# Loading a tap filter and k's first chunk ahead of ssm_k, and running two tap products during that load

## Chip, cores, metric

One core of one Trainium2 chip. Times are device microseconds of one execution (lower is better); a trace's own clock starts a little later, so the profiled spans are some 1.8 us shorter than the times. All ratios below compare runs on the same chip in the same rounds, and use only the runs whose state is fast (a run more than 1.5% above the fastest of its kernel counts as slow). Start times are read from one profiled execution of each kernel, some of them on different chips. The verdict "same" means within 2%.

## The reference, cut to what matters

```python
# S = 2048 tokens, D = 512 channels, 4 taps
k_shift[t] = sum over j of k[t - j] * shift_k[:, j]      # the tap filter
kv  = k_shift * v
y   = irfft( rfft(kv, 2S) * rfft(ssm_k, 2S) )[:S] + kv * ssm_D
h   = x + layernorm(x) * y                               # then an MLP with 512 -> 1376 -> 512
```

The kernel does the Fourier transforms as matmuls. `ssm_k` has to be transposed into rows (`kfl`) and put through a first DFT stage (into `a1k`); the tap filter is a product with diagonal matrices (`wdiag`) accumulated in PSUM, then multiplied by v in place (`vT`). Only when all of k·v is there can its own transposes begin. From there on this change touches nothing.

## The kernel before

```python
sk = ...;   nc.sync.dma_start(out=sk, in_=A_ssm_k)          # 2 MB, first on SP's ring
wsh = ...;  nc.scalar.dma_start(out=wsh, in_=A_shift_k)     # 4 KB, ACT's ring
for c in range(4):                                          # k and v, transposed by the DMA, behind ssm_k
    nc.sync.dma_start_transpose(out=kT[c], in_=k_d[...])
    nc.sync.dma_start_transpose(out=vT[:, :, ...], in_=v_d[...])
# ... cut: VectorE computes the angles of the sine tables (add, wrap), ScalarE the sines
for rg in range(4):                                         # GpSimd, when the filter is there
    nc.gpsimd.tensor_tensor(out=wdiag[:, rg], in0=ident, in1=wsh[:, rg], op=mult)

def to_rows(src, q, fl, eng):                # one group of 8 transposes, and its copy out of PSUM
    pst = psum.tile(...)                     # pool of four buffers, shared by all of the below
    for i in range(8):
        nc.tensor.transpose(out=pst[:, 0, i, :], in_=src[:, :, :, 8 * q + i], identity=ident)
    copy(eng, fl[:, :, :, 8 * q:8 * q + 8], pst[:, 0])

def taps(c, h):                              # one tap product: 8 matmuls of 512 columns, then times v
    ps = bank2("pkv")
    for i in range(2):
        for j in range(4):
            nc.tensor.matmul(out=ps[:, i, :], lhsT=wdiag[:, 2 * h + i, j, :], rhs=kT[c][...])
    nc.vector.tensor_tensor(out=vv, in0=ps, in1=vv, op=mult)

for q in range(8):
    to_rows(ssm_k, q, kfl, "DADADADA"[q])    # D: VectorE copies, A: ScalarE copies
for gb in range(8):                          # eight rounds
    taps(gb // 2, gb % 2)
    stage1(kfl, a1k, gb, ("AA", "AD")[gb % 2])   # 64 small matmuls, two evictions
    if gb in (0, 2, 4): cc_part()                # a sine table on ScalarE
# ... cut: the transposes of k·v and everything after
```

## Time and profile before

| | before |
|---|---|
| time, median of 3 runs | 221.04 us (220.21 to 221.72) |
| span of the profiled execution, mean granted TensorE clock | 218.5 us, 0.997 |
| first transpose of ssm_k / stage 1 / first transpose of k·v | 9.23 / 18.01 / 38.61 us |

The prediction shows the chain of waits and the loads. Three more views of this kernel are needed later: the page's shares of the chain that ended last, its row of the granted TensorE clock (one digit for a fortieth of the span, 9 is 90% or more), and, in the timeline, VectorE's work on the tables (start, duration, engine, line, operation).

```profile
PE 77%; DVE 11%; DMA 5%; ACT 2%; issue 2%; SPq 0%; DVEq 0%; ACTq 0%
```

```profile
PEclk9999999999999999999999999999999999999998
```

```profile
4.52 0.90 DVE L180 TENSOR_SCALAR w_ts<-w_ts 128x1408 int32<-128x1408 int32 x1
5.33 0.82 DVE L189 TENSOR_TENSOR w_ts<-w_ta 128x640 int32<-128x640 f32 x1
...
6.18 0.49 DVE L180 TENSOR_SCALAR w_ts<-w_ts 128x640 int32<-128x640 int32 x1
```

Of the 5% of DMA, 4% is the load of ssm_k (8.46 us). VectorE's tables run beside that load; they end at 9.35 + 1.23 = 10.58, and VectorE's first copy of kfl follows at 10.50 (neighbours overlap by a little). So VectorE is only just ready when the first eight transposes are.

### The profile page before, as it was taken

Reading aid. Unit: us, or ns where it says so; the run is one execution under the profiler, and the core shown is the slowest. Engines: PE = TensorE matmul, PEld = TensorE weight load, DVE = VectorE, ACT = ScalarE, POOL = GpSimd, SP = SyncE. Lnnn points to the kernel's source line nnn. Section 1 sums busy time; section 2 is a strip of 40 time slices with the busy share of each in tenths; the row PEclk is TensorE's granted clock in tenths of the full one; section 3 lists DMA queues with packets and bytes.
Section 4 is the critical chain, followed back from the end, with each engine's and each line's share of the span. In section 5 each row is a group of like instructions: output and inputs, shape, how many; then the busy total and the mean of one; then the engine's idle time right before and its main releaser. Section 6 shows DMA issues by size and latency. Waiting matters only on the chain.

```text
span 218.5 us, 5526 instructions
## 1 busy us (share of the span) xinstructions
PE 197.3 (90%) x2299; PEld 139.4 (64%) x2299; DVE 144.6 (66%) x226; ACT 116.6 (53%) x175; POOL 79.1 (36%) x120
## 2 busy tenths in 40 slices
PE   0389789999997999998999889999999999999992
PEld 0385444999986899995998844645646644444451
DVE  7975657886688899998495992976395480243031
ACT  2977847745598688884897128401550046106400
POOL 4299982000001899997648702100202001002000
PEclk9999999999999999999999999999999999999998
DMA  6999950000000004827941898594344430020012
GB/s 187 315 210 197 158 115 3 3 6 0 0 3 3 4 0 130 226 98 188 196 63 36 252 134 168 94 166 98 81 84 82 96 80 1 18 54 24 3 48 48
DMA packets 49512, 20.07 MB, mean 92 GB/s; under 512 B 44400, under 2 KB 47952, under 8 KB 49488
## 3 DMA queue, kind: packets, MB, share of 16 engines
q1 hardware_dynamic: 46816, 18.18, 40.7%
q10 hardware_dynamic: 2672, 1.54, 2.6%
q8 instruction: 18, 0.29, 0.5%
q14 instruction: 6, 0.05, 0.1%
HBM read 7.08 MB, written 2.10 MB: 42 GB/s over the span
## 4 chain that ended last, share of the span: by engine, by line
PE 77%; DVE 11%; DMA 5%; ACT 2%; issue 2%; SPq 0%; DVEq 0%; ACTq 0%
PE ps2m L603 18%; PE ps1m L586 18%; PE pkv L304 7%; PE psy L390 6%; PE pst L250 5%; PE pz L574 5%; DVE a1x L242 4%; DMA sk<-in_A_ssm_k_dram 4%; PE ps2k L282 3%; PE ps2k L284 3%; PE u L282 3%; PE u L284 3%; PE psi L510 3%; PE ps L266 3%; ACT ax L240 2%
## 5 line engine op out<-in xcount | busy, mean ns | idle before, releaser
L588 ACT ACTIVATE h1T<-ps1m 128x512 bf16<-128x512 f32 (+1 forms) x44 | 26.0, 596 | 56.2 <-PE ps1m L586 56.2
L586 PE MATMUL ps1m<-xT,w 128*128 128x512 bf16 (+1 forms) x176 | 39.0, 379 | 0.9 <-issue 0.6
L603 PE MATMUL ps2m<-w,h1T 128*128 128x512 bf16 (+3 forms) x187 | 39.4, 367 | 0.0
L606 DVE SCALAR_TENSOR_TENSOR o<-ps2m,rstd,xh 128x512 bf16<-128x512 f32 (+1 forms) x17 | 12.2, 719 | 32.3 <-PE ps2m L603 30.1
L586 PEld LDWEIGHTS <-w 128*128 128x128 bf16 (+1 forms) x176 | 17.4, 100 | 21.4 <-issue 1.1
L603 PEld LDWEIGHTS <-h1T 128*128 128x128 bf16 (+1 forms) x187 | 17.9, 98 | 19.2
L380 POOL TENSOR_TENSOR t<-usb,kf 128x320 fp32r<-128x320 f32 x32 | 28.3, 925 | 2.0 <-ACT usb L376 1.7
L380 DVE TENSOR_TENSOR t<-u,kf 128x704 fp32r<-128x704 f32 x32 | 26.7, 885 | 3.1 <-ACT usb L376 3.0
L460 POOL TENSOR_SCALAR rstd<-mv 128x4 f32<-128x4 f32 x8 | 2.3, 284 | 68.2 <-DVE mv L458 68.2
L456 DVE BATCH_NORM_STATS2 st<-xh 128x6 f32<-128x512 bf16 x32 | 19.7, 679 | 0.0
L240 ACT CAST kf<-psy 128x512 fp32r<-128x512 f32 x30 | 17.6, 645 | 2.0 <-PE psy L390 0.3
L574 PEld LDWEIGHTS pz<-ecore,ax 32*128 32x128 f32 x512 | 15.0, 186 | 3.4 <-issue 2.1
L574 PE MATMUL pz<-ecore,ax 32*128 32x128 f32 (+7 forms) x512 | 15.8, 273 | 1.1 <-ACT ax L240 1.1
L556 DVE TENSOR_TENSOR qT<-pz,qT 128x1024 bf16<-128x1024 f32 x8 | 9.8, 1223 | 10.5 <-PE pz L574 6.6
L390 PE MATMUL psy<-t,ipos 128*128 128x512 f32 x48 | 16.0, 393 | 0.0
L240 ACT CAST a1k<-ps 128x1024 fp32r<-128x1024 f32 x12 | 12.4, 1071 | 6.3 <-PE ps L266 6.3
L510 PE MATMUL psi<-dre,kf 128*128 128x256 f32 x64 | 15.5, 286 | 0.0
L250 PE MATMUL pst<-ident,sk 128*128 128x128 bf16 x64 | 6.5, 276 | 9.8 <-DMA sk<-in_A_ssm_k_dram 9.2
L304 PE MATMUL pkv<-kT,wdiag 128*128 128x512 bf16 x64 | 15.2, 381 | 0.0
L510 PE MATMUL psi<-dim,kf 128*128 128x256 f32 x64 | 15.2, 280 | 0.0
L240 ACT CAST ax<-psi 128x1024 fp32r<-128x1024 f32 x13 | 12.4, 1019 | 4.6 <-DVE st L456 3.0
L307 DVE TENSOR_TENSOR vT<-pkv,vT 128x1024 bf16<-128x1024 f32 x8 | 9.8, 1224 | 7.0 <-PE pkv L304 6.8
(115 smaller groups left out, 396.8 us busy)
## 6 DMA issues: line engine op xcount, KB each, us to landing
sk<-in_A_ssm_k_dram SPq DMA_DIRECT2D x1, 2048.0 KB, 8.5
xh<-in_A_q_dram SPq DMA_DIRECT2D x16, 128.0 KB, 3.0
out_dram<-o SPq DMA_DIRECT2D x60, 32.0 KB, 1.6
w<-in_B_w_dram SPq DMA_DIRECT2D x1, 1376.0 KB, 6.4
w<-in_B_w_dram ACTq DMA_DIRECT2D x1, 1280.0 KB, 6.3
xh<-xT SPq DMA_TRANSPOSE x8, 3.2
w<-in_B_w_dram ACTq DMA_DIRECT2D x1, 96.0 KB, 6.2
kT<-in_A_k_dram SPq DMA_TRANSPOSE x4, 6.1
```

The source lines that it names most:

```text
L240: nc.scalar.copy(out=o, in_=i)
L250: nc.tensor.transpose(out=pst[:, 0, i, :], in_=src[:, :, :, 8 * q + i], identity=ident[:])
L282: nc.tensor.matmul(out=ps[:, kk, :], lhsT=at_k1(w_re, k1), rhs=a_in[:, k1, :], start=True, stop=False, skip_group_check=True)
L304: nc.tensor.matmul(out=ps[:, i, :], lhsT=wdiag[:, 2 * h + i, j, :], rhs=kT[c][:, 2 * h + i, 16 - j:CH + 16 - j], start=(j == 0), stop=(j = ...
L380: eng.tensor_tensor(out=t[:, :, j, :], in0=in0.unsqueeze(1).to_broadcast([P, 2, n, 2]), in1=kfr[:, :, j, ks], op=ALU.mult)
L390: nc.tensor.matmul(out=psy[:], lhsT=m_[:], rhs=t_.rearrange("p j k -> p (j k)"), start=first, stop=not first)
L456: nc.vector.bn_stats(out=st[:, i, :], in_=src[:, i, :])
L510: nc.tensor.matmul(out=ps[:, i // 2, i % 2, :], lhsT=kf[:, c, 4 * m:4 * m + 4, :].rearrange("p r k -> p (r k)"), rhs=d[:].rearrange("p d a ...
L574: nc.tensor.matmul(out=pz[:, rg, 32 * jl:32 * (jl + w)], lhsT=ax[rows, 64 * rho + n2, :, :].rearrange("p d g -> p (d g)"), rhs=ecore[q][ro ...
L586: nc.tensor.matmul(out=ps1[:fsz, :].rearrange("p (i t) -> p i t", i=4), lhsT=w1[:, c, fc * P:fc * P + fsz], rhs=hT[sc][:, :, c, :], start= ...
L588: nc.scalar.activation(out=h1T[:fsz, fc, :], in_=ps1[:fsz, :], func=ACT.Relu)
L603: nc.tensor.matmul(out=ps2[:, 0:w], lhsT=h1T[:ksz, fc, i * P:(i + 1) * P], rhs=w2[:ksz, fc, ds], start=(fc == 0), stop=(fc == NFC - 1))
```

## The change

TensorE is idle until ssm_k has landed. The intent is to use that time: bring the filter (4 KB) and k's first chunk (512 KB) in before ssm_k, run that chunk's two tap products while ssm_k loads, park them in SBUF (`ahead`), and multiply them with v later from there. Two of the eight tap products, 1.84 us each, should so leave the critical path.

```diff
-    nc.sync.dma_start(out=sk[:], in_=A_ssm_k...)
-    nc.scalar.dma_start(out=wsh[:], in_=A_shift_k...)
+    nc.sync.dma_start(out=wsh[:], in_=A_shift_k...)
         if c == 0:
             nc.sync.dma_start_transpose(out=kT[c][:, :, 16:CH + 16], in_=k_d[0:CH, :])
+            nc.sync.dma_start(out=sk[:], in_=A_ssm_k...)
# GpSimd: wdiag right after ident (before: after the two memsets f2hi, f2lo)
+    ahead = slotA.tile([P, DC, CH], F32, tag="A", name="ahead")
+    for h in range(2):
+        nc.scalar.copy(out=ahead[:, 2 * h:2 * h + 2, :], in_=taps_mm(0, h))
     for q in range(8):
         to_rows(skv, q, kfl, "DADADADA"[q])
+        if q in (4, 6):
+            taps_mul(ahead[:, q - 4:q - 2, :], 0, q // 2 - 2)
     for gb in range(8):
-        taps(gb // 2, gb % 2)
+        if gb >= 2:
+            taps_mul(taps_mm(gb // 2, gb % 2), gb // 2, gb % 2)
         stage1(kfl, a1k, gb, ("AA", "AD")[gb % 2])
```

(`taps_mm` and `taps_mul` are the two halves of `taps`. The cut says in words what moved on GpSimd.)

More of the change, by code (lines that the diff above doesn't have):

```diff
@@ L94 @@
     sk = early.tile([P, DC, S], BF16, name="sk")
-    nc.sync.dma_start(out=sk[:], in_=A_ssm_k.rearrange("(c p) t -> p c t", p=P))
     wsh = consts.tile([P, DC, KS], BF16, name="wsh")
-    nc.scalar.dma_start(out=wsh[:], in_=A_shift_k.rearrange("(r p) j -> p r j", p=P))
+    nc.sync.dma_start(out=wsh[:], in_=A_shift_k.rearrange("(r p) j -> p r j", p=P))
     dtab = consts.tile([P, 64, DC], BF16, name="dtab")
@@ L111 @@
             nc.sync.dma_start_transpose(out=kT[c][:, :, 16:CH + 16], in_=k_d[0:CH, :])
+            nc.sync.dma_start(out=sk[:], in_=A_ssm_k.rearrange("(c p) t -> p c t", p=P))
         else:
@@ L153 @@
                             base=0, pattern=[[-1, P]], channel_multiplier=1)
+    for rg in range(DC):
+        nc.gpsimd.tensor_tensor(out=wdiag[:, rg, :, :], in0=ident[:].unsqueeze(1).to_broadcast([P, KS, P]),
+                                in1=wsh[:, rg, :].unsqueeze(2).to_broadcast([P, KS, P]), op=ALU.mult)
     n1c = early.tile([P, 1], F32, name="n1c")
@@ L219 @@
         nc.gpsimd.memset(f[:], 0.0)
-    for rg in range(DC):
-        nc.gpsimd.tensor_tensor(out=wdiag[:, rg, :, :], in0=ident[:].unsqueeze(1).to_broadcast([P, KS, P]),
-                                in1=wsh[:, rg, :].unsqueeze(2).to_broadcast([P, KS, P]), op=ALU.mult)
     nc.gpsimd.tensor_copy(out=f1hi[:, 0:64], in_=f1f[:])
@@ L285, in stage2, with taps_mm, taps_mul @@
                              skip_group_check=True)
+    def taps_mm(c, h):
+        ps = bank2("pkv")
+        for i in range(2):
+            for j in range(KS):
+                nc.tensor.matmul(out=ps[:, i, :], lhsT=wdiag[:, 2 * h + i, j, :],
+                                 rhs=kT[c][:, 2 * h + i, 16 - j:CH + 16 - j], start=(j == 0), stop=(j == KS - 1))
+        return ps[:]
+    def taps_mul(src, c, h):
+        vv = vT[:, 2 * h:2 * h + 2, CH * c:CH * c + CH]
+        nc.vector.tensor_tensor(out=vv, in0=src, in1=vv, op=ALU.mult)
+    ahead = slotA.tile([P, DC, CH], F32, tag="A", name="ahead")
+    for h in range(2):
+        nc.scalar.copy(out=ahead[:, 2 * h:2 * h + 2, :], in_=taps_mm(0, h))
     kfl = early.tile([P, 64, 2, 64], BF16, name="kfl")
@@ L297 @@
     a1k = slotA.tile([P, 64, 256], F32R, tag="A", name="a1k")
-    def taps(c, h):
-        ps = bank2("pkv")
-        for i in range(2):
-            for j in range(KS):
-                nc.tensor.matmul(out=ps[:, i, :], lhsT=wdiag[:, 2 * h + i, j, :],
-                                 rhs=kT[c][:, 2 * h + i, 16 - j:CH + 16 - j], start=(j == 0), stop=(j == KS - 1))
-        vv = vT[:, 2 * h:2 * h + 2, CH * c:CH * c + CH]
-        nc.vector.tensor_tensor(out=vv, in0=ps[:], in1=vv, op=ALU.mult)
     for gb in range(8):
-        taps(gb // 2, gb % 2)
+        if gb >= 2:
+            taps_mul(taps_mm(gb // 2, gb % 2), gb // 2, gb % 2)
         stage1(kfl, a1k, gb, ("AA", "AD")[gb % 2])
```

## The prediction

> **What bounds the kernel now.** I read the chain of work that ended last first, in order of time, because it says which work of the start is on the path. Columns: start, duration (us), what.
>
> ```profile
> 0.72 8.46 DMA sk<-in_A_ssm_k_dram
> 9.23 4.25 PE pst L250 x40
> 13.51 1.24 DVE kfl L242
> 14.79 1.56 PE pst L250 x16
> 16.35 1.73 PE pkv L304 x8
> 18.08 0.61 PE ps L266 x64
> 18.70 1.84 PE pkv L304 x8
> ...
> 26.14 1.76 issue
> ...
> 37.33 1.24 DVE vT L307
> 38.61 6.01 PE pst L250 x64
> ```
>
> Everything waits for ssm_k until 9.2. Then come 64 transposes of it (L250), then eight rounds of tap products (pkv, L304) and the first DFT stage (ps, L266), then at 38.61 the transposes of k·v. From there on the program is unchanged and TensorE is its chain nearly throughout (PE 90% busy on the page; loads wait for PE, not PE for loads), so I count what the change does to the time 38.61 and carry that to the end one to one. One round takes 1.84 + 0.61 = 2.45 us with TensorE never idle, except once: 1.76 us of "issue" near 26.
>
> Next the list of DMA issues (last column: us from issue to landing) and the timeline of the start.
>
> ```profile
> sk<-in_A_ssm_k_dram SPq DMA_DIRECT2D x1, 2048.0 KB, 8.5
> kT<-in_A_k_dram SPq DMA_TRANSPOSE x4, 6.1
> wsh<-in_A_shift_k_dram ACTq DMA_DIRECT2D x1, 4.0 KB, 8.8
> ```
>
> ```profile
> 1.25 7.79 SPq L111 DMA_TRANSPOSE kT<-in_A_k_dram  x1
> 9.64 4.85 POOL L222 TENSOR_TENSOR wdiag<-ident,wsh 128x512 bf16<-128x512 bf16 x4 [6.34 <-DMA wsh<-in_A_shift_k_dram]
> 10.50 1.21 DVE L242 COPY kfl<-pst 128x1024 bf16<-128x1024 bf16 x1
> 13.51 1.22 DVE L242 COPY kfl<-pst 128x1024 bf16<-128x1024 bf16 x1 [0.20 <-PE pst L250]
> 16.39 1.01 ACT L240 COPY kfl<-pst 128x1024 bf16<-128x1024 bf16 x1 [1.13 <-PE pst L250]
> 18.76 1.99 ACT L240 CAST a1k<-ps 128x1024 fp32r<-128x1024 f32 x2 [1.36 <-PE ps L266]
> 20.62 1.25 ACT L184 ACTIVATE c2c<-w_tc,hbi,hsc 128x1024 fp32r<-128x1024 int32 x1
> ```
>
> The tap filter (4 KB) arrives only with ssm_k, and k's first chunk, stuck behind ssm_k, lands at 1.25 + 10.2 = 11.45 (the 10.2 is the largest landing time in the view of tile kT). So today no tap product can run early. But the first tap product (16.35) already covers a wait: the last copy of kfl ends only at 16.39 + 1.01 = 17.40, and stage 1 needs all of kfl. It costs about 18.08 - 17.5 = 0.5 us, not 1.73.
>
> **What the Trainium skill says.** (1) "DMA: Bandwidth & Descriptors", Queues, rings and completion order: each DMA engine serves one ring in order and takes turns between rings. The trace agrees: the 4 KB filter on ACT's ring landed 8.8 us after issue, beside ssm_k's 8.5. Put first on SP's ring the filter is early, and k's chunk really goes ahead of ssm_k. (2) "TensorE: Matmul & The Clock Gate", Part 1: an idle array starts at 1.2 GHz, 426.7 ns per 512-column matmul, for at least about 3.4 us. In this trace warm tap matmuls go at 1.84/8 = 230 ns; the first 40 transposes took 106 ns each, and the 64 later ones 6.01/64 = 94, which is compatible but no proof. (3) "Advanced Engine Details and Errata", ISA Cache: 256 instructions a line, two lines. The trace has an instruction queue with 18 packets of 16 KB, one of them in 25 to 26 us, just ahead of the 1.76 us "issue" gap; I read that gap as a late instruction block. (4) "GPSIMD Engine Reference", 1. Specifications: GpSimd shares SBUF access with VectorE. One wdiag product beside a VectorE operation took 1840 ns, the others 1035.
>
> **The change part by part.**
>
> *a. Loads.* Bytes ahead of ssm_k grow by k's chunk (512 KB). The same two transfers were both done at 11.45 before, so with the order turned round ssm_k lands at about 11.5: by rates, the DMA windows show 0.39 MB/us for ssm_k and at best 0.29 for transposes, so 0.52/0.29 = 1.8 us for the chunk and 0.5 to 0.7 us for the small filter and D packets, 9.2 + 2.4 = 11.6. Cost: +2.3 us. All later transposes stay where they are: the total of bytes ahead of them is the same (about 2.7 us each, the last landing at 24.5 + 5.4 = 30).
>
> *b. The early tap products.* The filter lands near 3, wdiag is four products of 1.03 to 1.84 us, so done at 7.5 to 9; k's chunk lands near 6. Sixteen matmuls warm are 3.7 us, cold 6.8. I take 10 to 12 cold ones: 12 x 0.427 + 4 x 0.23 = 6.0, ending near 12.0. So TensorE, not ssm_k, may be what starts the transposes, at about T = 12.0. That is +2.8 against 9.23. ScalarE's two copies (1.0 each) fall to 11 to 13, then the table (1.25); kfl copies wait little for that.
>
> *c. Transposes of ssm_k.* They went from 9.23 to stage 1 at 18.01, 8.8 us. After: the built program's waits show that groups 2, 4 and 6 each wait for VectorE's copy of the group two before (the early tap products hold two of the four PSUM buffers when these groups are assigned). One such step is copy 1.22 + transposes 0.8 + hand-overs 0.15 = 2.17 us (13.51 to 15.68 in the trace is one). So: first copy at T + 1.0, third group's copy at T + 5.4, ended T + 6.6; now the first multiplication with v (1.22 us, as for the PSUM form at L307) stands in VectorE's queue ahead of the copy of group 6, which runs T + 7.85 to T + 9.1. The last ScalarE copy ends about T + 9.45. Stage 1 starts at T + 9.5 = 21.5. Before it was 18.01: +3.5 in all.
>
> *d. The rounds of stage 1.* Two tap products are gone (each 1.84 us of TensorE), but ScalarE's and VectorE's evictions take over at the head. From stage 1's start t0, with copies of 1.0 (ACT), 1.22 (DVE), table 1.15: first two evictions end t0 + 2.75, table 3.9, third 4.9. Tap product of round 2 waits for the first (1.8, ends 3.7), stage 1 of round 2 follows (ends 4.35), tap product of round 3 waits for the eviction at 4.9. That is 0.6 + 0.6 us of new idle time on TensorE. From round 3 on it is again 2.45 to 2.55 a round: stage 1 of round 7 starts at t0 + 16.95, the last multiplication with v ends at t0 + 18.4. Before, without the issue gap: 38.61 - 18.01 - 1.76 = 18.85. So only 0.4 us of the 1.84 is gained here, since ScalarE (12 copies and 3 tables, 15.8 us) is nearly as long as TensorE (6 x 1.84 + 8 x 0.61 = 15.9).
>
> *e. The issue gap.* The instruction block is needed at the same place in the program, the end of round 3. From the start of round 2 to there it had 3.2 us before and took 5; now it has about 3.7, and fewer transposes are still in flight. I put the gap at 0.6 of 1.76 (0 to 1.8).
>
> Sum: transposes of k·v start at 12.0 + 9.5 + 18.4 + 0.6 = 40.5, against 38.61: +1.9 us. 221.04 + 1.9 = 222.9.
>
> **The rivals.** *R1, the intended one:* tap products are free under the load, ssm_k is delayed little, and 2 x 1.84 us or a bit more vanish. For it: TensorE, idle until 9.23, has the room. Against it: the 0.5 MB must go through the same 16 DMA engines, busy 90% in the second slice of the page. It would give 217.5 to 219. *R2: the load order decides* and costs more than is won, my view: +1.9. *R3: cold TensorE and crowded GpSimd.* wdiag comes only at 9 to 10 and all sixteen matmuls run cold; transposes start at 13.5 to 14 and the whole is 225 to 226. For it: the 1840 ns product and VectorE being busy 2 to 10.5 us. Against: GpSimd has nothing else to do from 3.3 to 9.6. *R4: the issue gap as it was, or gone:* +-1 us around any of these. *R5: the load is hidden anyway,* the multiplications from SBUF fall into VectorE's idle time and all is a draw: 221.
>
> **Range and chances.** Uncertain are T (+-0.9), the copies' order (+-0.5), the gap (+-0.8), and runs (220.2 to 221.7 before). Together about 1.6 us for 8 in 10, widened a little downward for R1: 220.5 to 225.0. Over 2% faster is below 216.6, which needs more than even R1 gives: 0.02. Over 2% slower is above 225.5, R3 with the gap: 0.07. Within: 0.91.
>
> **What would show it.** Right if ssm_k lands near 11.5 and its first transpose starts at 11.5 to 12.5; a tap matmul takes about 0.43 us at first; the multiplication stands ahead of group 6's copy; stage 1 starts near 21.5; TensorE has two gaps of about 0.6 us before rounds 2 and 3; the k·v transposes start near 40.5 and everything later is shifted by the same amount. Wrong if ssm_k lands before 10.5 (R1), if wdiag ends after 9.5 (R3), if the first two rounds of stage 1 don't wait for ScalarE, or if the shift at the k·v transposes is not the shift at the end, in which case a later stage has slack I did not see.

## The result, and the profile after

| | before | after | predicted |
|---|---|---|---|
| median (range), 4 runs each | 221.38 us (220.21 to 221.87) | 223.75 us (223.52 to 223.98) | 222.9 (220.5 to 225.0) |
| profiled span, mean granted clock | 218.5 us, 0.997 | 222.0 us, 0.992 | |
| ssm_k's first transpose | 9.23 | 12.30 | 12.0 |
| stage 1 starts | 18.01 | 21.91 | 21.5 |
| k·v's first transpose | 38.61 | 42.09 | 40.5 |

The ratio is 1.0115 (95% interval 1.0071 to 1.0159): slower by about 1%, verdict "same". Ratios here and below are the mean time of one kernel's fast runs over that of the other's of the same rounds, so not quite the ratio of the quoted medians. From k·v's first transpose to the end both traces take 179.9 us, so all of the 3.5 us between the two traces arises in the first 42 us.

First the page's shares of the chain that ended last and its clock row, of the kernel after.

```profile
PE 80%; DVE 15%; issue 2%; ACT 2%; POOL 0%; DVEq 0%; POOLq 0%; ACTq 0%
```

```profile
PEclk9999799999999999999999999999999999999999
```

The load has gone from the chain, and VectorE's share rose from 11 to 15%. The fifth slice (22.2 to 27.8 us) ran at a reduced TensorE clock. The chain in order of time (start, duration, what) shows where:

```profile
2.75 1.75 DVE w_ts L192
...
12.42 1.23 DVE w_tc L183
13.65 1.14 DVE kfl L242
...
14.84 0.87 PE pst L250 x8
...
21.91 1.10 PE ps L266 x51
...
24.13 2.44 PE pkv L292 x8
...
29.90 1.49 issue
```

Before, the chain began with "DMA sk". Now, after some small operations of GpSimd and VectorE, it runs along VectorE's tables until the first copy of kfl at 13.65. ssm_k came late too, but what started the copies last was VectorE. Then come steps of a VectorE copy and eight transposes (14.84, and again at 17.01), then stage 1 and a tap product that takes 2.44 us (1.84 before) in the slice of the low clock, and an issue gap of 1.49.

From the list of DMA issues (last column: us from issue to landing), and from the timeline, one line each:

```profile
sk<-in_A_ssm_k_dram SPq DMA_DIRECT2D x1, 2048.0 KB, 8.6
```

```profile
6.19 6.28 PE L292 MATMUL pkv<-kT,wdiag 128*128 128x512 bf16 x16 [6.19 <-DMA kT<-in_A_k_dram]
```

ssm_k was issued at 3.58 (the timeline has that line too) and landed at 3.58 + 8.6 = 12.2; the filter took 2.0 us, where it took 8.8 before. The sixteen early matmuls really ran under the load, from 6.19 to 12.47, but cold: their weight loads start every 0.43 us.

Last, the timeline of GpSimd and VectorE at the start, after (queried in narrow windows, so that the four products show one by one; here in order of start):

```profile
2.75 1.74 DVE L192 TENSOR_TENSOR w_ts<-w_ta 128x1408 int32<-128x1408 f32 x1
3.10 2.29 POOL L155 TENSOR_TENSOR wdiag<-ident,wsh 128x512 bf16<-128x512 bf16 x1
4.53 1.61 DVE L183 TENSOR_SCALAR w_ts<-w_ts 128x1408 int32<-128x1408 int32 x1
5.36 1.68 POOL L155 TENSOR_TENSOR wdiag<-ident,wsh 128x512 bf16<-128x512 bf16 x1
6.06 1.66 DVE L192 TENSOR_TENSOR w_ts<-w_ta 128x640 int32<-128x640 f32 x1
7.00 1.62 POOL L155 TENSOR_TENSOR wdiag<-ident,wsh 128x512 bf16<-128x512 bf16 x1
7.75 1.21 DVE L183 TENSOR_SCALAR w_ts<-w_ts 128x640 int32<-128x640 int32 x1
8.58 1.28 POOL L155 TENSOR_TENSOR wdiag<-ident,wsh 128x512 bf16<-128x512 bf16 x1
...
13.57 1.22 DVE L242 COPY kfl<-pst 128x1024 bf16<-128x1024 bf16 x1
```

Read the ends, start plus duration: VectorE 4.49, GpSimd 5.39, VectorE 6.14, GpSimd 7.04, VectorE 7.72, GpSimd 8.62, VectorE 8.96, GpSimd 9.86. They alternate strictly, and each GpSimd product ends 0.90 us after the VectorE operation ahead of it. I read this as the two engines taking turns, whole instruction by whole instruction, so that an operation's duration in the trace includes its wait for the other engine. This is how VectorE's wrap went from 0.90 to 1.61 us, the add from 0.82 to 1.66, the second wrap from 0.49 to 1.21, and a small one after them from 0.23 to 1.01: +3.05 us in all, and the first copy of kfl came at 13.57 instead of 10.50, +3.07. It fits the Trainium skill, "SBUF — State Buffer", Who interferes with whom: there a VectorE instruction in a 2-port mode, or one with two SBUF inputs beside a GpSimd one that reads SBUF, contends with GpSimd, and the one that issues second "fully blocks". Before, wdiag came after 9.64, when most of VectorE's table work was done: only its first product met a table operation (it took 1.84 us and ended at 11.48, again 0.90 after that operation's end at 10.58), the other three took 1.03 each, and VectorE's copies out of PSUM beside them kept their 1.21 to 1.23 us.

### The profile page after: what moved, and what is told of

The parts are those of the page before. It is cut to its first block, busy times and chain, and to the rows that moved or that the text cites. A ratio compares the mean times of both kernels' runs of the same rounds, so it can differ in the third digit from the quotient of the medians.

```text
span 222.0 us, 5528 instructions
## 1 busy us (share of the span) xinstructions
PE 201.2 (91%) x2299; PEld 141.1 (64%) x2299; DVE 147.5 (66%) x226; ACT 118.8 (54%) x177; POOL 83.8 (38%) x120
## 4 chain that ended last, share of the span: by engine, by line
PE 80%; DVE 15%; issue 2%; ACT 2%; POOL 0%; DVEq 0%; POOLq 0%; ACTq 0%
PE ps2m L612 17%; PE ps1m L595 17%; PE psi L519 7%; PE psy L399 7%; PE pz L583 5%; PE pkv L292 5%; DVE a1x L242 4%; PE pst L250 4%; PE ps2k L282 3%; PE ps2k L284 3%; PE u L282 3%; PE u L284 3%; PE ps L266 3%; DVE kfl L242 2%; DVE w_ts L192 2%
## 5 line engine op out<-in xcount | busy, mean ns | idle before, releaser
L615 DVE SCALAR_TENSOR_TENSOR o<-ps2m,rstd,xh 128x512 bf16<-128x512 f32 (+1 forms) x17 | 12.2, 719 | 32.0 <-PE ps2m L612 29.2
L292 PE MATMUL pkv<-kT,wdiag 128*128 128x512 bf16 x64 | 18.2, 439 | 6.5 <-DMA kT<-in_A_k_dram 6.2
L292 PEld LDWEIGHTS <-wdiag 128*128 128x128 bf16 x64 | 6.6, 109 | 15.1 <-POOL wdiag L155 5.4
L240 ACT CAST a1k<-ps 128x1024 fp32r<-128x1024 f32 x12 | 12.4, 1073 | 5.4 <-PE ps L266 5.4
```

Of the source, the lines that this page charges most:

```text
L240: nc.scalar.copy(out=o, in_=i)
```

## The experiments

Twelve runs were made, in three batches, each batch on one chip. "Stage 1" and "k·v" are start times in the profiled execution.

| run | base and edit | stage 1 | k·v | median us | ratio to before (95%) |
|---|---|---|---|---|---|
| a0_after_again | after, unaltered | 22.4 | 42.4 | 223.6 | 1.0136 (1.0089, 1.0182) |
| e1_order_only | before, load order alone | 21.7 | 43.9 | 223.49 | 1.0142 (1.0091, 1.0192) |
| e2_free_load | after, ssm_k not behind k | 22.2 | 41.8 | 222.95 | 1.0112 (1.0067, 1.0157) |
| e5_filter_early | before, filter early alone | 21.96 | 41.8 | 222.82 | 1.0062 (1.0031, 1.0093) |
| e3_buffers | after, PSUM buffers in turn | 20.38 | 40.2 | 221.94 | 1.0049 (1.0026, 1.0071) |
| e4_round0 | after, ScalarE relieved | 22.4 | 41.8 | 224.23 | 1.0178 (1.0129, 1.0227) |
| c1_no_waits | e3, multiplications last | 19.55 | 40.1 | 222.27 | 1.0067 (1.0040, 1.0094) |
| c2_keep_warm | c1, 12 idle matmuls | 20.2 | 40.9 | 223.5 | 1.0117 (1.0064, 1.0171) |
| p1_before_pad | before, 15 idle transposes | 17.8 | 36.89 | 219.47 | 0.9963 (0.9935, 0.9990) |
| a1_after_pad | after, 15 idle matmuls | 22.16 | 43.1 | 226.22 | 1.0261 (1.0201, 1.0320) |
| c3_no_waits_pad | c1, 28 idle matmuls | 20.27 | 38.17 | 221.8 | 1.0051 (1.0027, 1.0075) |
| p2_before_warm | before, 58 idle transposes | 17.8 | 37.67 | 223.12 | 1.0105 (1.0059, 1.0152) |

The theories: **(A)** the load order sets the start; **(B)** something else would hold the start even with a free load; **(C)** the assignment of PSUM buffers costs a wait in every second group; **(D)** ScalarE holds the first rounds; **(E)** the issue gap is a late block of instructions, tied to a place in the program.

### The change again, on another chip

> The changed kernel again, unaltered, so that the two padded runs have it beside them on the same chip: ratio to before 1.008 to 1.015, first transpose of k*v at 41.5 to 42.5, issue gap at the end of round 3 between 0.9 and 1.8 us.

1.0136, beside 1.0115 in the first measurement. The first one was no accident, and all six runs again had a mean clock below full (see below).

### A against B: the loads

**e1_order_only.** The kernel before, with the order of loads alone.

```diff
-    nc.sync.dma_start(out=sk[:], in_=A_ssm_k...)
-    nc.scalar.dma_start(out=wsh[:], in_=A_shift_k...)
+    nc.sync.dma_start(out=wsh[:], in_=A_shift_k...)
             nc.sync.dma_start_transpose(out=kT[c][:, :, 16:CH + 16], in_=k_d[0:CH, :])
+            nc.sync.dma_start(out=sk[:], in_=A_ssm_k...)
```

> The kernel before with the new load order alone (filter first, k's first chunk ahead of ssm_k); no early tap products, wdiag at its old place. If the load order is the cost: ssm_k's first transpose at about 12.2 us, 8.8 us to stage 1 as before, first transpose of k*v near 41.4 (before 38.61, after 42.09), time about 2.8 us above before (ratio 1.013), so at or above the changed kernel. If the load order is hidden by something else (rival): ratio 1.000 to 1.004. If the early tap products win much and only the load order loses (rival), this run is more than 2 us above the changed kernel.

Transposes of ssm_k start at 12.62, and the kernel is 1.4% slower than before, about 3.1 us: as slow as the whole change. So the new order of loads is enough for the whole cost, and the early tap products won back nothing that the times show. But this edit also brings the filter early, so it does not tell A from B: wdiag ran from 3.29, and VectorE's wrap took 1.61 us here too. (The profiled execution was the slowest of the six, 225.43 us, so its k·v start of 43.9, for 41.4 expected, overstates the delay.)

**e2_free_load.** The whole change, but with ssm_k right behind the filter. The early tap products then have no k to read, so they read a constant tile; they are the same matmuls with wrong values, on purpose (the output stayed within the tolerance, which says nothing here).

```diff
     nc.sync.dma_start(out=wsh[:], in_=A_shift_k...)
+    nc.sync.dma_start(out=sk[:], in_=A_ssm_k...)
+    kfake = kvp.tile([P, 256], BF16, name="kfake");  nc.vector.memset(kfake[:], 0.125)
...
-                                 rhs=kT[c][:, 2 * h + i, 16 - j:CH + 16 - j], ...)
+                                 rhs=kfake (broadcast to 512 columns) if c == 0 else kT[c][...], ...)
```

> Wrong result on purpose: the changed kernel with ssm_k issued ahead of k's first chunk again and the early tap products reading a constant tile, so they cost no load. The load order as the only cost would give a first transpose of ssm_k at 9.5 and a time near 221.0, some 2.7 us below the changed kernel. My theory is that TensorE, cold, is nearly as late as the load: early products from 5.5 (wdiag) for 16 x 0.43 us, end near 12, so ssm_k's transposes start at 11.7 to 12.3 and the time is only 0 to 0.7 us below the changed kernel.

Taking ssm_k's delay away gained nothing: ratio 1.0112 (all six runs at a mean clock of 0.985 or less), and stage 1 at 22.2. In its timeline the transposes wait for VectorE instead:

```profile
13.91 1.22 DVE L244 COPY kfl<-pst 128x1024 bf16<-128x1024 bf16 x1
...
15.18 1.60 PE L252 MATMUL pst<-ident,sk 128*128 128x128 bf16 x16 [1.78 <-DVE kfl L244]
```

They started at 11.83, when the cold tap products were done, and after two groups stood 1.78 us until VectorE had copied. Three bounds lie side by side at the start: the load (12.2) and cold TensorE (11.8 to 12.4), each with about 1 us of transposes still to come before the first copy, and VectorE, free for that copy at 13.6. Taking the load away leaves the others.

**e5_filter_early.** To see the third alone: the kernel before, with the filter early on SP's ring and ssm_k right behind it. The instructions on the compute engines are those of before; wdiag only runs earlier.

```diff
-    nc.sync.dma_start(out=sk[:], in_=A_ssm_k...)
-    nc.scalar.dma_start(out=wsh[:], in_=A_shift_k...)
+    nc.sync.dma_start(out=wsh[:], in_=A_shift_k...)
+    nc.sync.dma_start(out=sk[:], in_=A_ssm_k...)
```

> The kernel before with one change: the 4 KB filter is issued first on SyncE's queue, ahead of ssm_k. k's chunk stays behind ssm_k, the instructions of every engine are the same. The four wdiag products on GpSimd then run from about 3 us, beside VectorE's table arithmetic, instead of from 9.6. Theory (found after the prediction): they slow that arithmetic by some 3 us, as in the changed kernel, so VectorE's first copy of kfl starts near 13.6 instead of 10.5, stage 1 near 20 to 20.5 instead of 18.0, and the time is 1.5 to 2.5 us above before though ssm_k still lands by 9.8. Rival (only the late ssm_k costs): same as before within 0.6 us.

```profile
10.20 3.65 PE L250 MATMUL pst<-ident,sk 128*128 128x128 bf16 x32 [10.20 <-DMA sk<-in_A_ssm_k_dram]
...
13.58 3.54 DVE L242 COPY kfl<-pst 128x1024 bf16<-128x1024 bf16 x3
```

VectorE's wrap takes 1.61 us here too and the first copy starts at 13.58, the same as after the whole change, although the transposes begin at 10.20 and no tap product runs early. Stage 1 starts at 21.96, and the kernel is 0.6% slower, 1.4 us. (Stage 1 was expected at 20 to 20.5; the tap product ahead of it took 2.99 us for 1.73 before, after TensorE had waited.) So wdiag beside VectorE's tables is a bound of its own, and B is right: A alone falls. No run has the new load order without this delay of VectorE, so what the load order costs by itself was not measured. (The filter ahead also pushed ssm_k from 9.23 to 10.20.)

### C and D: buffers, ScalarE

**e3_buffers.** The whole change, with the four PSUM buffers handed out by hand in turn, in place of the pool's choice.

```diff
+    TAKE = [0, 1, 2, 3] * 4 + [1, 0, 2, 3] * 14
+    def slot(): return dict(tag=f"ps{TAKE.pop(0)}", bufs=1) if TAKE else dict(tag="ps")
-        return psum.tile([P, 2, 512], F32, tag="ps", name=name)
+        return psum.tile([P, 2, 512], F32, name=name, **slot())
-        pst = psum.tile([P, 2, 8, P], BF16, tag="ps", name="pst")
+        pst = psum.tile([P, 2, 8, P], BF16, name="pst", **slot())
```

> The changed kernel with the four PSUM buffers handed out in turn, so that groups 2 and 3 of the transposes of ssm_k wait for the early tap products' copies and groups 4 and 6 for VectorE's copies of groups 0 and 2, instead of each even group for the copy of the group just two before. Everything later keeps its waits. Theory (the chain of copy, transposes, copy at 2.19 us a step sets the start of stage 1): stage 1 at about 20.0 instead of 21.9, time 1.5 to 2 us less than the changed kernel. Rival (the multiplication with v standing in VectorE's queue sets it): stage 1 within 0.4 us of 21.9.

```profile
12.39 5.93 PE L256 MATMUL pst<-ident,sk 128*128 128x128 bf16 x64 [1.44 <-DMA sk<-in_A_ssm_k_dram]
...
21.76 1.97 ACT L246 CAST a1k<-ps 128x1024 fp32r<-128x1024 f32 x2 [2.40 <-PE ps L272]
```

All 64 transposes now run as one stretch of 5.93 us; in the kernel after they took from 12.30 to 20.8. Stage 1 starts 1.5 us earlier, k·v 1.9 earlier, and the ratio is 1.0049 over 22 runs. C is right: by the ratios (1.0049 beside 1.0115 and 1.0136) the change loses 1.5 to 1.9 us to something that is no part of its idea. (The issue gap is also smaller here, 0.34 for 1.49, so not all of the 1.9 at k·v need be the buffers'.) Two smaller losses show up: the multiplication with v takes 1.78 us here and stands ahead of group 6's copy, which ends only at 20.28; and the first eviction of stage 1 came only at 21.76. It writes `a1k` into the memory of `ahead`, which the second multiplication was still reading until 21.68; c1 below tests this.

**e4_round0.** The whole change, with the second eviction of the first round given to VectorE and the three tables moved later.

```diff
-        stage1(kfl, a1k, gb, ("AA", "AD")[gb % 2])
-        if gb in (0, 2, 4):
+        stage1(kfl, a1k, gb, "AD" if gb < 2 else ("AA", "AD")[gb % 2])
+        if gb in (2, 4, 5):
```

> The changed kernel with round 0 of stage 1 evicted by ScalarE and VectorE instead of ScalarE alone, and the three tables after rounds 2, 4 and 5 instead of 0, 2 and 4. Theory (ScalarE is what TensorE waits for in rounds 2 and 3): the idle times of about 0.6 us before round 2's and round 3's tap products shrink, from stage 1's start to the first transpose of k*v 19.2 to 19.7 instead of 20.2, time 0.5 to 1.0 us less. Rival (the cold clock and the late instruction block make all of the 20.2): same as the changed kernel within 0.3 us.

From stage 1 to k·v it took 19.4 us, where the kernel after took 20.2; but 0.6 of the 0.8 is a smaller issue gap (0.89 for 1.49), and the times are no better (1.0178, verdict "unclear" as the interval passes 2%; all six runs had a mean clock of 0.985 or less). D is not supported.

**c1_no_waits.** e3, and the multiplications with v behind all eight groups, from a tile that no stage-1 eviction waits for.

```diff
-    ahead = slotA.tile([P, DC, CH], F32, tag="A", name="ahead")
+    ahead = the tile of the last cosine table, seen as [P, DC, CH]
-        if q in (4, 6):
-            taps_mul(ahead[:, q - 4:q - 2, :], 0, q // 2 - 2)
+    for h in range(2):                                  # after the loop over q
+        taps_mul(ahead[:, 2 * h:2 * h + 2, :].bitcast(F32), 0, h)
```

> The changed kernel with the buffers of run e3, the two early multiplications with v after all copies of kfl in VectorE's queue, and the early products kept in a table's space instead of the slot of the first stage's result. In e3 VectorE's last copy stood behind a multiplication until 19.07 and the first eviction of stage 1 waited for the second multiplication until 21.76. Theory: stage 1 starts at 19.4 to 19.7 (e3 20.4), its first eviction 0.8 us later, first transpose of k*v near 38.8 to 39.5 (e3 40.2); time about 1 us below e3, near before. Rival (these waits are hidden behind ScalarE or the load): within 0.3 us of e3.

Stage 1 starts at 19.55, 0.8 earlier than in e3, and its first eviction comes 0.75 after that instead of 1.4. k·v started at 40.1, only 0.03 earlier than in e3, and the time did not follow either (1.0067; about 1 us less was expected). Its chain shows where the gain went:

```profile
23.47 0.86 issue
...
27.40 2.04 issue
```

Two issue gaps, 2.9 us together, where the kernel after has one of 1.49 and e3 one of 0.34 in its rounds.

### E: the issue gap

Counted in the programs as built, the matmul after such a gap has the index 706 in TensorE's instructions in before, 707 in after, 451 and 707 in c1, 962 in p2: 256 apart but for one or so. If a gap belongs to a block of 256 instructions, adding instructions ahead of it must move it to earlier work by just so many.

**p1_before_pad.** Fifteen transposes of the identity (30 instructions of TensorE: a weight load and a matmul each) into an unused half of the first group's buffer.

```diff
         pst = psum.tile([P, 2, 8, P], BF16, tag="ps", name="pst")
+        if src is skv:
+            for i in range(15 if q == 0 else 0):
+                nc.tensor.transpose(out=pst[:, 1, i % 8, :], in_=ident[:], identity=ident[:])
```

> The kernel before with fifteen transposes of the identity put in front of TensorE's work, in its idle time, written to an unused half of a PSUM tile: thirty instructions more, all done by about 5 us. If the issue gap near 26 us is a late block of instructions, the boundary moves thirty instructions forward, from the end of round 3 of stage 1 into the tap product before it, and the block that has to be fetched lasts about 4.7 us instead of 3.2: gap 0 to 0.5 us instead of 1.76, time 1 to 1.7 us below before. If the gap is tied to the time and not to the place in the program (rival), it stays 1.2 to 1.8 us and the time is that of before.

Its chain, in the fourth round and much later:

```profile
25.51 0.47 PE ps L269 x47
25.98 0.10 issue
26.08 0.30 PE ps L269 x17
```

```profile
124.25 1.84 issue
```

And late in the chain of the kernel before:

```profile
127.79 0.63 issue
```

In the kernel before, the gap stood after 62 of the round's 64 matmuls; here a small gap stands after 47, exactly the 15 earlier. So E is right about the place. The gap shrank from 1.76 to 0.10 there, k·v started at 36.89 (1.72 earlier), and the kernel is the only one of all that beats both: 0.9963 over 22 runs, some 0.8 us, with the verdict "same" (1 to 1.7 us were expected). A part was lost again in a later gap, 1.84 us at 124.25 where before has 0.63 at 127.79. All fourteen traces have this later gap. Counted again in TensorE's instructions, two to a matmul, the one after it has an index of 3266 to 3269 in every trace: ten blocks of 256 after 706. It is 0.48 to 0.77 us in the nine without padding, and 1.63 to 2.51 in the five with it (p1, a1, c2, c3, p2).

**a1_after_pad, c3_no_waits_pad, p2_before_warm.** Does padding cure it in general?

```diff
# a1 (on after: 15) and c3 (on c1: 28), ahead of the first tap product
+        for _ in range(15 if c == h == 0 else 0):
+            nc.tensor.matmul(out=ps[:, 0, 0:P], lhsT=ident[:], rhs=ident[:], start=True, stop=True)
# p2: as p1
-            for i in range(15 if q == 0 else 0):
+            for i in range(58 if q == 0 else 0):
```

> The changed kernel with fifteen 128-column matmuls of the identity in TensorE's idle time ahead of the early tap products, overwritten by them: the instruction blocks move by thirty. Theory (as in p1_before_pad): the gap at the end of round 3 falls from 1.5 to below 0.5 us and the time by 0.8 to 1.5 us against the unaltered changed kernel, and the loss against the padded kernel before stays 2 to 3 us. Rival: the gap stays, and so does the time.

> c1 (buffers, multiplications and slot mended) with 28 such matmuls in front: blocks moved by 56, TensorE busy from 3 us. c1 had issue gaps of 0.86 and 2.04 us in rounds 2 and 3. Theory: both go to below 0.5, stage 1 starts at 19.3 to 19.7, first transpose of k*v at 37.2 to 38.0; time 1.5 to 2.5 us below c1, so 0.5 to 1.5 us below before but still 0.3 to 1.5 us above the padded kernel before. Rival (the change wins once its waits are gone): below p1_before_pad.

> The kernel before with 58 such transposes from 3 us to about 9 us, so TensorE enters the transposes of ssm_k at full clock, and blocks moved by 116. If the clock mattered there: stage 1 at 17.2 to 17.6 instead of 17.8 to 18.0 and a time 0.3 to 0.7 us below p1_before_pad. If copies set the pace (rival): same as p1_before_pad within 0.3 us. The issue gap should be below 0.5 us in both cases.

No. In its rounds a1 has only a gap of 0.62, but it came between two ScalarE evictions and a tap product of which six matmuls then took 2.76 us on a slow clock (mean 0.975 over its runs); a gap of 1.71 followed at 130.5, and it was the one kernel with the verdict "slower". c3 lost all gaps in its rounds and started k·v at 38.17, but then had one of 1.74 at 126, with a lower clock beside it, and ended no earlier than e3. p2 has one of 1.04 in its fifth round and one of 2.51 at 123.8. Its other question, whether TensorE at full clock would shorten the transposes, is answered no in its one trace: stage 1 started at 17.8, as in p1.

Padding moves the gaps about, and in these traces it made the later one longer. c3 and p2 also refute a part of my reckoning: there the shift at k·v is not the shift at the end (k·v to end 182.8 us in c3, 183.7 in p2, against 179.9).

**c2_keep_warm.** c1, with twelve matmuls of the identity ahead of the first stage-1 block, to keep TensorE busy in its wait and so the clock up.

```diff
         pss = [bank2("ps1") for _ in range(2)]
+        for _ in range(12 if fl is kfl and gb == 0 else 0):
+            nc.tensor.matmul(out=pss[0][:, 0, 0:P], lhsT=ident[:], rhs=ident[:], start=True, stop=True, ...)
```

> c1 with twelve extra 128-column matmuls of the identity in TensorE's idle time ahead of stage 1, overwritten by it; they also move the instruction blocks by 24. If idle time ahead of stage 1 lets TensorE's clock fall (granted 0.7 in 21.9 to 27.5 of the changed kernel), rounds 0 and 1 take 1.22 instead of 1.35 to 1.7 us and the next tap product 1.84 instead of 2.4: 0.5 to 1 us below c1. Rival: the clock falls anyway or does not matter, within 0.3 us of c1.

1.0117, slower than c1. It decides nothing: the 24 instructions moved a gap of 1.64 us into the first tap product of the rounds, and the mean clock of its runs, 0.995, hardly differs from c1's 0.994.

### The clock, from all runs together

The kernel before ran 109 times in the three batches. 75 runs had a mean granted clock of 0.995 or more, all of them fast, and took 220.36 us on average; the other 34 had about 0.992 and took 222.23 (the 20 fast ones among them 221.94). So its runs fall into two groups by clock, 1.6 to 1.9 us apart. The ten timed runs of the kernel after all had a clock below 0.993 and took 223.67 on average: 3.3 us more than before at full clock, near the 3.5 that the two traces differ by. Runs of p1 had 0.998 on average. Part of the cost is there at full clock too: of the runs at 0.995 or more, five of e1 took 223.39 on average and thirteen of e5 222.27, where before on the same chips took 220.49 and 220.33.

## Why the prediction was right

The time is in its range and the direction and the verdict hold; the total came out 0.85 us too low. By its own steps:

**Step a, the load order: right, a little small.** ssm_k landed at 12.2 instead of 9.18, +3.0 for the +2.3 predicted.

**Step b, cold tap products: right.** 0.43 us a matmul, and T = 12.30 for 12.0. wdiag was done at 9.86, later than the 7.5 to 9 of the text and in the window that rival R3 named; it is one of the prediction's own signs of being wrong ("if wdiag ends after 9.5"). The matmuls wait only for their own quarter of it, so it did not hold them.

**Missing from a to c: VectorE.** The prediction quoted the contention of GpSimd and VectorE and took from it only what GpSimd loses. It had counted VectorE as ready at T + 1.0 = 13.0. VectorE lost 3.05 us by taking turns, and the first copy came at 13.57. Because ssm_k and TensorE were late by nearly as much, this added at most about half a microsecond; but it means that the reason given, the load order, is only one of three. e2 and e5 show it: R2 was right on the sign, and wrong that the load order decides. That steps a to c came out so near (21.91 for 21.5) is therefore partly luck: a delay that the prediction did not count would by itself have put stage 1 at 21.96 (e5).

**Step c, the copies of every second group: right.** The step was 2.17 us (14.84 to 17.01) as worked out, and stage 1 came at T + 9.6 for T + 9.5. e3 shows that the buffers are the cause. In the kernel after, the multiplication ahead of group 6's copy cost about 0.1 us.

**Step d, the rounds: the sum nearly right, the reason wrong.** 20.18 us from stage 1 to k·v, less the gap of 1.49, is 18.69 for 18.4. But of the two waits of 0.6 us for ScalarE, named as a sign of being right, only one of 0.32 appeared. In their place the first two stage-1 blocks, which now run back to back, took 1.7 us (their weight loads 1.74) instead of 2 x 0.61, and the tap product after the first of them 2.44 instead of 1.84, in the stretch with the granted clock of 0.70. Relieving ScalarE (e4) did not help.

**Step e, the issue gap: mis-sized.** 1.49 for 0.6. That is the largest single error of the sum, 0.9 us, though within the stated 0 to 1.8.

**The account closes so.** Predicted +1.9 at k·v; measured +3.5 in the traces, of which 0.9 is step e, 0.3 step d, and 0.4 the later start of stage 1. The times differ by less (2.4 us between the medians), because many runs of the kernel before also fall into a low clock, while the trace of before was taken at full clock. Added to the 221.04 that the prediction started from, 3.5 would have made 224.5, so that the time came within 0.85 us of the forecast is in part luck too. What stays open: why the clock falls. In the stretch of ssm_k's transposes TensorE was busy 6.39 of 9.60 us after and 8.19 of 8.80 before, and the low clock followed that idling; but this is only argued, as the one test of it (c2) moved a gap as well, and before and c1 stood 1.76 and 2.04 us in their gaps with no fall in their clock rows. Why some instruction blocks come late and others not is open too.

## What to carry to other kernels

Filling an idle engine is worth only what the next bound leaves: before moving work under a load, list every engine that must be ready when the load ends, and by how much each is early; here VectorE was early by nothing, and moving GpSimd's products beside it was alone enough to put stage 1 as late (21.96 in e5) as the whole change did (21.91). When tiles from a shared pool are allocated earlier, look which buffer each later tile now gets, as here a wait in every second group came from that. And differences of 1% in a program this long are within what a late instruction block or a window of low clock makes: test with several padded copies of both kernels before believing such a gain, since one padding by itself moved the time by -0.4% (p1), +1.1% (p2) and +1.2% (a1 beside a0).

## What the Trainium skill lacked or had wrong

- "Advanced Engine Details and Errata", ISA Cache, gives the block of 256 instructions, but neither it nor another page gives a time for a block that comes late: TensorE stood 0.1 to 2.5 us at places that lie whole multiples of 256 apart (1.76 in before, 0.86 and 2.04 in c1, 2.51 in p2), and 30 instructions more moved the border by exactly 15 matmuls and shrank the stall from 1.76 to 0.10.
- "TensorE: Matmul & The Clock Gate", Part 1, puts the warm-up at under 1% of a typical span and advises against fitting it. What the clock makes here is of that size (1.6 to 1.9 us of 221), but it is about half of the effect of this whole change or more: it splits the runs of one kernel into two groups (220.36 and 222.23 us), so a mean clock beside each run belongs into every comparison of this size.
- "GPSIMD Engine Reference", 1. Specifications, names the contention in one row of a table; it does not say there that the second instruction waits for the whole of the first, and so that VectorE pays as well (the page of SBUF named above does). Here VectorE lost 3.05 us, and four GpSimd products took 6.76 us, where one that met no such VectorE operation took 1.03 (before).
